# Moving eight small copies of v and halving one block transfer at the start of a fused attention and feed-forward kernel

## The chip, the cores and the metric

The kernel runs on one core of one Trainium2 chip. The metric is the device time of one execution in microseconds (us); the median of several executions is compared. TensorE (PE in the profile) multiplies matrices, VectorE is DVE, ScalarE is ACT, GpSimd is POOL, and SyncE (SP) issues nearly all DMA transfers. Each engine works through its own list of instructions in order and waits at an instruction until what it needs is there.

## The reference

Two blocks follow each other. The first is attention over 8 batches and 8 heads, with 576 positions of 64 numbers, in which every score that lies more than `tau` under the maximum of its row is dropped. The second is a feed-forward block on the 4608 resulting rows of 512 numbers.

```python
scores = scale * np.matmul(q, k.transpose(0, 1, 3, 2))
thresh = np.max(scores, axis=-1, keepdims=True) - tau
scores = np.where(scores >= thresh, scores, -1000000000.0)
attn = softmax(scores)                     # exp, divided by the sum of the row
attn_out = np.matmul(attn, v)              # (8, 8, 576, 64)
x = attn_out.transpose(0, 2, 1, 3).reshape(4608, 512)
h = x @ w_in                               # (4608, 1024), w_in arrives as 64-bit numbers
solu = h * softmax(h)
ln = (solu - mean) / sqrt(var + 1e-6) * g_ln
out = ln @ w_out                           # (4608, 512)
```

## The kernel before

**Rounds.** The attention is cut into 144 rounds (`slots`, 18 for each batch). A round handles 128 rows of scores for the two heads of a pair. Two rounds (r = 0 and r = 1) with the same batch, kind and pair `hp` make one unit; unit 0 is rounds 0 and 1, unit 1 is rounds 2 and 3, and unit 3, the fourth, is rounds 6 and 7. For one round the work passes over all engines:

- PE computes the scores of two heads into two banks of PSUM (`s_ps`, line 504), which are free only when the round before has been read.
- DVE finds the threshold of each row (line 526, result `nth`), once for each head.
- ACT turns the scores into differences from that threshold (line 541, called the ramp here) and takes the exponential with its row sum (line 550).
- One round later POOL normalises: two small operations on the sums (lines 557 and 558) and two multiplications of 128x576 (line 560). DVE then transposes the two results in blocks of 32x32 into `T` (line 571).
- When both rounds of a unit are transposed, SP sends `T` to `wT` in three transfers (`spread`, lines 592 and 594), which put the 32-row blocks on the partitions that the next product wants. `wT` has two buffers.
- Some rounds later PE multiplies `wT` with v (line 631, 72 matmuls), and ACT copies the result out of PSUM (line 664). These products fall due at fixed rounds: unit 0 in round 6, unit 1 in round 7, unit 2 in round 9, unit 3 in round 10.

**Weights.** Beside this, the first seventeen rounds convert the weights from 64-bit numbers piece by piece: a load on SP's queue (line 279), a scaled copy of the upper words (line 294 on ACT, or 298 on POOL or DVE), a mask on DVE (line 303), a conversion of the lower words on ACT (line 306), a merge on DVE (line 318) and an addition on POOL (line 328). Tables of numbers say in which round and at which of its places each of these is written.

**Order.** The program is written out by hand: `tc.manual_schedule()` keeps each engine's instructions in the order in which the code emits them. A round has places: its beginning (phase 0, ahead of its scores and thresholds), phase 1 (behind its exponentials), phase 2 (behind the normalisation of the round before) and its end (phase 3). `weigh(phase)` emits what the tables give for the number 4 * round + phase.

**Copies of v.** For batch 0 the product needs v twice: the upper half of the partitions also needs what the lower half holds, and the other way round. So 64 partitions times 2 heads times 256 numbers are copied across, in eight copies numbered 0 to 7: copies 0 and 1 serve unit 0, copies 2 and 3 unit 1, copies 4 and 5 unit 2, copies 6 and 7 unit 3. `VAT` gives the place of each copy and `VBY` its engine (0 is ACT, line 187; 1 is DVE, line 189; 2 is POOL, line 191).

```python
to = halves[b, hf]["v"][ROWS[r], 2 * pr : 2 * pr + 2, 4:8]
of = halves[b, hf]["v"][ROWS[1 - r], 2 * pr : 2 * pr + 2, 0:4]
if by == 0:
    nc.scalar.copy(out=to, in_=of)
elif by == 1:
    nc.vector.tensor_scalar(out=to, in0=of, scalar1=1.0, scalar2=None, op0=ALU.mult)
else:
    nc.gpsimd.tensor_scalar(out=to, in0=of, scalar1=1.0, scalar2=1.0, op0=ALU.mult, op1=ALU.mult)
```

**Halves of a unit.** From round 29 on (`START` is 30) `blocks` does not wait for the second round of a unit: it sends the half of r = 0 one place after the next round's exponentials, and the half of r = 1 when that is transposed. Before round 29 the whole unit is sent at once.

Of the kernel before, what the change touches and what calls it, by code (L numbers as in the profile page):

```python
# [20 lines left out]
def kernel(  # L21
# [161 lines left out]
    def copy_v(b, hf, pr, r, by):  # L183
# [7 lines that stand above are left out]
            nc.gpsimd.tensor_scalar(  # L191
                out=to, in0=of, scalar1=1.0, scalar2=1.0, op0=ALU.mult, op1=ALU.mult
            )
# [370 lines left out]
    def blocks(s):  # L564
        b, kind, hp, r = slots[s]
        key = (b, kind, hp)
        if r == 0:
            units[key] = dict(T=work.tile([P, 2, 2, NK, 2, 32], F32, tag="T", name="T"))
        T = units[key]["T"]
        for h, w in enumerate(live.pop(s)["w"]):  # L570
            nc.vector.transpose(  # L571
                out=T[:, :, r, :, h, :], in_=w.rearrange("p (c m x) -> p c m x", c=2, x=32)
            )
        if r == 1 or s >= START - 1:
            if r == 1:
                spread(key)
            else:
                jobs(MORE, s + 1, spread=lambda: spread(key, (0,)))

    def spread(key, rs=(0, 1)):  # L580

        kind = key[1]
        u = units[key]
        rs = [r for r in rs if r not in u.setdefault("spread", [])]
        if not u["spread"]:
            u["wT"] = work.tile([P, 2, 2, NK, 2, 32], F32, tag="wT", bufs=2, name="wT")
        u["spread"] += rs
        T = u["T"].rearrange("p c r m h x -> p c (r m h x)")
        to = u["wT"].rearrange("p g r m h x -> p g (r m h x)")
        rs = slice(64 * NK * rs[0], 64 * NK * (rs[-1] + 1))  # L590
        if kind < 2:
            nc.sync.dma_start(out=to[:, 1, rs], in_=T[32:96, :, rs])
            for half in range(2):
                nc.sync.dma_start(
                    out=to[ROWS[half], 0, rs], in_=T[96 * half : 96 * half + 32, :, rs]
                )
            return
        for g in range(2):
            for half in range(2):
                of = 64 * half + 32 * g  # L600
                nc.sync.dma_start(out=to[ROWS[half], g, rs], in_=T[of : of + 32, :, rs])
# [355 lines left out]
        "turn": (1, 0),  # L957
    }
    SPLIT = {30: 0, 32: 30, 34: 6, 36: 5, 38: 16, 40: 30, 42: 7, 44: 23, 46: 11}
    LATER, KEPT = 47, (3, 4)  # L960
    SEVEN = {0: 21, 1: 21, 2: 24, 3: 25, 5: 25, 4: 26, 7: 26, 6: 29}
    PIECE = {0: (-1, 1, 3, 6, 7, ), 1: (-1, 3, 5, 10, 11, ), 2: (-1, 8, 11, 14, 15, ), 3: (3, 12, 15, 18, 19, ), 4: (4, 15, 18, 21, 25, ), 5: (7, 20, 23, 26, 27, ), 6: (11, 23, 25, 30, 31, ), 7: (13, 27, 31, 34, 35, ), 8: (23, 31, 35, 38, 39, ), 9: (23, 35, 39, 42, 43, ), 10: (29, 39, 43, 46, 47, ), 11: (35, 43, 47, 50, 51, ), 12: (39, 49, 51, 54, 55, ), 13: (43, 52, 55, 58, 59, ), 14: (43, 55, 59, 62, 63, ), 15: (55, 59, 63, 66, 67, )}
    RAW = {0: 0, 1: 1, 2: 2, 3: 3, 4: 0, 5: 1, 6: 2, 7: 3, 8: 0, 9: 1, 10: 2, 11: 3, 12: 0, 13: 1, 14: 2, 15: 0}
    QUEUE = {0: 1, 1: 0, 2: 0, 3: 0, 4: 0, 5: 0, 6: 0, 7: 0, 8: 0, 9: 0, 10: 0, 11: 0, 12: 0, 13: 0, 14: 0, 15: 0}
    UNIT = {0: 0, 1: 2, 2: 2, 3: 2, 4: 1, 5: 2, 6: 1, 7: 1, 8: 1, 9: 0, 10: 1, 11: 1, 12: 1, 13: 1, 14: 0, 15: 0}
# [6 lines left out]
    LAG = {1: 2, 3: 1, 5: 1, 9: 1, 11: 1, 17: 0, 21: 0, 23: 1, 25: 1}  # L972
    FETCH = {0: 10, 1: 8, 2: 8, 3: 11, 4: 15, 5: 15, 6: 13, 7: 17, 8: 17, 9: 19, 10: 21, 11: 25, 12: 0, 13: 0, 14: 3, 15: 5}
    VHALF = (0, 1)
    VAT = {0: 15, 1: 15, 2: 19, 3: 19, 4: 31, 5: 31, 6: 34, 7: 34}
    VBY = {0: 2, 1: 2, 2: 2, 3: 2, 4: 0, 5: 0, 6: 0, 7: 0}
    LOAD2 = {0: 20, 1: 17, 2: 24, 3: 21, 4: 31, 5: 31, 6: 32, 7: 34}
    TURN2 = {0: 23, 1: 24, 2: 27, 3: 28, 4: 33, 5: 34, 6: 36, 7: 37}
    ENDS2 = {0: 30, 1: 28, 2: 42, 3: 44}
# [6 lines left out]
    def jobs(table, r, **do):  # L986
        for name, (phase, n) in table.items():
            if name in do:
                when = (begin, early, middle, late)[phase].setdefault(r + n, [])
                when.insert(0 if name in ("attended", "out") else len(when), do[name])  # L990
# [254 lines left out]
    START = 30  # L1245
# [70 lines left out]
    with tc.manual_schedule():  # L1316
# [40 lines left out]
        for x in range(NW):  # L1357
            def copies(x):
# [5 lines left out]
                (weight_load, weight_a, weight_b, weight_c, weight_gain, copies),  # L1364
                (*PIECE[x], MOVE.get(x, PIECE[x][4])),
            )
            for n, job, when in jobs_of:
                weights.setdefault(when, []).append((n, x, job))

        for x, when in VAT.items():  # L1370
            of = 0, VHALF[x // 4], x // 2 % 2, x % 2
            weights.setdefault(when, []).append(
                (6, x, lambda _, of=of, by=VBY[x]: copy_v(*of, by))
            )
# [85 lines left out]
        def attend_some(n):  # L1460
            key, steps = pv[0]
            if sum(1 for _ in zip(range(n), steps)) < n or n > 144:
                pv.clear()
                jobs(MORE, rnd, attended=lambda: done_with(key))

        def steady_round(due):
# [46 lines left out]
        while True:  # L1513
# [71 lines left out]
            if rnd - 1 in live:  # L1585
                blocks(rnd - 1)
# [47 lines left out]
```

## Time and profile before

| | |
|---|---|
| median of 3 runs | 846.54 us (844.78 to 851.36) |
| the profiled execution | 848.12 us, its span 846.3 us |
| PE busy | 799.6 us, 94% of the span |
| DVE, ACT, POOL busy | 674.5, 605.0, 574.2 us |
| HBM read, written | 45.09 MB, 9.44 MB |

The profile lists for each engine how long it was busy; its views show groups of instructions, windows of time, the instructions in order of time (the timeline) and the chain of work that ended last, followed back from the end. In the timeline a row starts with the start and the length in us, then come engine, line, operation, the tile that is written and the tile that is read, and a count; a bracket says how long the engine had been idle just before and whose result ended that. A row with a count merges several instructions of one kind. "issue" is idle time in which the engine waited for nothing that the profile shows. SPq rows are the times in which SP issues a transfer, not the transfer itself.

### The profile page before, as it was taken

How to read it: one execution, taken by the hardware profiler on the slowest of the kernel's cores; microseconds unless marked ns; L12 is line 12 of the kernel's file. 1: busy time of each engine (PE TensorE's matmuls, PEld its weight loads, DVE VectorE, ACT ScalarE, POOL GpSimd, SP SyncE). 2: the span in 40 equal slices, each digit the busy share in tenths (PEclk: the TensorE clock that was granted, in tenths of full speed). 3: DMA queues.
4: the chain of work that ended last, by engine and by line, in shares of the span. 5: the costliest groups of instructions: out<-in, count | busy, mean ns of one | idle time of the engine just before them, and what ended most of it. 6: DMA issues, size and time to landing. Idle time of an engine off the chain costs nothing.

```text
span 846.3 us, 36895 instructions
## 1 busy us (share of the span) xinstructions
PE 799.6 (94%) x15345; PEld 554.4 (66%) x15345; DVE 674.5 (80%) x1323; ACT 605.0 (71%) x1218; POOL 574.2 (68%) x1036
## 2 busy tenths in 40 slices
PE   5569889999999999999999999999999999999997
PEld 3346667766665666666777876666676876666556
DVE  5799869878789698979798698979688888787362
ACT  6799868767777686878686787778586687876231
POOL 4979767866867667677766768686666768574330
PEclk9789999999999999999999999999999999999999
DMA  8989788988787687968787677877687666555122
GB/s 252 256 219 253 189 204 212 236 222 211 220 244 216 174 224 211 242 190 218 205 230 208 195 207 220 231 206 199 192 218 222 180 183 201 150 138 139 42 52 52
DMA packets 99768, 166.40 MB, mean 197 GB/s; under 512 B 18504, under 2 KB 47184, under 8 KB 99600
## 3 DMA queue, kind: packets, MB, share of 16 engines
q1 hardware_dynamic: 98688, 162.95, 71.1%
q8 instruction: 121, 1.98, 1.0%
q10 hardware_dynamic: 912, 1.08, 0.5%
q14 instruction: 47, 0.39, 0.1%
HBM read 45.09 MB, written 9.44 MB: 64 GB/s over the span
## 4 chain that ended last, share of the span: by engine, by line
PE 82%; ACT 5%; POOL 3%; DMA 3%; issue 3%; DVE 2%; SPq 1%; DVEq 0%; POOLq 0%; ACTq 0%
PE ov L1195 22%; PE h L747 17%; PE s_ps L504 15%; PE ov L631 13%; PE o_ps L1195 6%; PE h L771 5%; ACT w L541 2%; PE h_ps L1061 2%; DMA wT<-T 2%; DMA v<-in_v_dram 1%; ACT w L550 1%; POOL w L560 1%; PE pv L631 1%; DVE w L526 1%; PE s_ps L372 1%
## 5 line engine op out<-in xcount | busy, mean ns | idle before, releaser
L541 ACT ACTIVATE w<-s_ps,nth 128x576 f32<-128x576 f32 x282 | 199.6, 741 | 141.4 <-DVE nth L526 136.2
L526 DVE CUSTOM_DVE_ANT_0 w<-s_ps,tau_t 128x576 f32<-128x576 f32 x282 | 201.4, 750 | 51.8 <-PE s_ps L504 40.7
L560 POOL TENSOR_SCALAR w<-w,sm 128x576 f32<-128x576 f32 x288 | 214.6, 757 | 14.3
L1195 PE MATMUL ov<-w,uT 64*64 64x256 f32 x3456 | 220.5, 379 | 2.8 <-issue 2.8
L571 DVE STREAM_TRANSPOSE T<-w 128x576 f32<-128x576 f32 x288 | 207.4, 755 | 19.2 <-POOL w L560 18.4
L550 ACT ACTIVATE w<-w,ntau 128x576 f32<-128x576 f32 x288 | 219.7, 768 | 0.0
L504 PE MATMUL s_ps<-kT,qT 64*64 64x512 f32 (+1 forms) x2048 | 174.8, 418 | 20.1 <-ACT w L541 17.9
L1195 PEld LDWEIGHTS ov<-w,uT 64*64 64x64 f32 x3456 | 158.3, 134 | 49.1 <-issue 13.6
L631 PEld LDWEIGHTS ov<-wT,v 64*64 64x64 f32 x4752 | 132.6, 133 | 33.5 <-issue 18.7
L631 PE MATMUL ov<-wT,v 64*64 64x128 f32 (+1 forms) x4752 | 137.6, 259 | 0.2
L557 POOL TENSOR_SCALAR sm<-sm 128x2 f32<-128x2 f32 x144 | 45.9, 319 | 134.9 <-ACT w L550 130.3
L558 POOL TENSOR_TENSOR sm<-sm,mone 128x2 f32<-128x2 f32 x144 | 103.5, 719 | 12.0
L504 PEld LDWEIGHTS s_ps<-kT,qT 64*64 64x64 f32 x2048 | 72.0, 137 | 51.0 <-ACT w L541 23.7
L747 PE MATMUL h<-w,xh 64*64 64x512 f32 x832 | 103.4, 593 | 0.5 <-POOL mark L110 0.4
L1150 DVE TENSOR_SCALAR u<-u,rs,nb 128x1024 f32<-128x1024 f32 x31 | 29.8, 961 | 49.6 <-ACT V L1144 49.6
L1195 PE MATMUL o_ps<-w,uT 64*64 64x256 f32 x1088 | 65.5, 377 | 0.8 <-ACT xh L664 0.5
L747 PEld LDWEIGHTS h<-w,xh 64*64 64x64 f32 x832 | 38.6, 133 | 40.5 <-issue 23.1
L1195 PEld LDWEIGHTS o_ps<-w,uT 64*64 64x64 f32 x1088 | 49.1, 133 | 19.1 <-issue 5.2
L550 ACT ACTIVATION_READ_ACCUMULATOR w<-w,ntau 128x1 f32 x288 | 55.7, 193 | 0.0
L1177 DVE STREAM_TRANSPOSE uT<-V 128x1024 f32<-128x1024 f32 x36 | 44.0, 1221 | 14.2 <-DMA V<-u 4.9
L747 PE MATMUL h<-k,sum 64*64 64x512 f32 x312 | 50.6, 589 | 0.0
L1144 ACT ACTIVATE V<-u,nb,rs 128x1024 f32<-128x1024 f32 x36 | 44.7, 1241 | 5.2 <-POOL nb L1122 5.2
(134 smaller groups left out, 1017.0 us busy)
## 6 DMA issues: line engine op xcount, KB each, us to landing
wT<-T SPq DMA_DIRECT2D x132, 288.0 KB, 4.8
wT<-T SPq DMA_DIRECT2D x256, 144.0 KB, 4.0
out_dram<-ob SPq DMA_DIRECT2D x71, 128.0 KB, 4.3
V<-u SPq DMA_DIRECT2D x136, 64.0 KB, 2.0
wT<-T SPq DMA_DIRECT2D x14, 576.0 KB, 5.5
q<-in_q_dram SPq DMA_DIRECT2D x24, 288.0 KB, 4.6
q<-in_k_dram SPq DMA_DIRECT2D x24, 288.0 KB, 4.5
v<-in_v_dram SPq DMA_DIRECT2D x12, 576.0 KB, 5.6
```

What stands on the lines that cost most here:

```text
L504: nc.tensor.matmul(out=ps[h][ROWS[y], ks], lhsT=lhsT, rhs=d["kT"][ROWS[h], ks], start=True, stop=True,)
L526: nc.vector.tensor_tensor_reduce(out=w, in0=ps[:, 0:S], in1=(zero if loose else tau_t).to_broadcast([P, S]), scale=1.0, scalar=BIG, op0=AL ...
L541: nc.scalar.activation(out=d["w"][x], in_=d["w"][x] if d["loose"] else d["ps"][x][:, 0:S], func=AF.Prelu, bias=d["nth"][x], scale=-1.0, al ...
L550: nc.scalar.activation(out=w, in_=w, func=AF.Exp, bias=ntau, scale=1.0, accum_out=sm[:, x : x + 1])
L557: nc.gpsimd.tensor_scalar(out=sm, in0=sm, scalar1=1e-9, scalar2=None, op0=ALU.add)
L558: nc.gpsimd.tensor_tensor(out=sm, in0=sm, in1=mone, op=ALU.pow)
L560: nc.gpsimd.tensor_scalar(out=w, in0=w, scalar1=sm[:, x : x + 1], scalar2=1.0, op0=ALU.mult, op1=ALU.mult)
L571: nc.vector.transpose(out=T[:, :, r, :, h, :], in_=w.rearrange("p (c m x) -> p c m x", c=2, x=32))
L631: nc.tensor.matmul(out=to, lhsT=d["v"][ROWS[u], (h0 + h - u) % 4 if b > 1 else h0 + h, m ^ 4 * u if m < 8 and b < 2 else m,], rhs=rhs, sta ...
L747: mm = nc.tensor.matmul(out=h[ROWS[y], 512 * bank : 512 * bank + 512], lhsT=x[ROWS[r], ROWS[y]], rhs=w[ROWS[r]], start=c == 0 and (n, r, k ...
L1144: nc.scalar.activation(out=V, in_=u, func=AF.Identity, bias=nb, scale=rs)
L1195: nc.tensor.matmul(out=to[ROWS[z], 0:256], lhsT=d["uT"][ROWS[r], m].rearrange("p y x -> p (y x)"), rhs=w2[ROWS[r], m ^ r, 256 * z : 256 * ...
```

## The change

Two things change. The eight copies get other places and partly other engines (`VAT`, `VBY`), and a unit whose first round is in `SOONER` (round 6, which is the fourth unit, unit 3) is sent in two halves, as the later units are. In `PIECE` only trailing commas go. Nothing else moves.

| copy | serves unit | before | now |
|---|---|---|---|
| 0 | 0 | POOL, end of round 3 | DVE, beginning of round 3 |
| 1 | 0 | POOL, end of round 3 | ACT, round 2, phase 1 |
| 2 | 1 | POOL, end of round 4 | DVE, beginning of round 4 |
| 3 | 1 | POOL, end of round 4 | POOL, end of round 3 |
| 4 | 2 | ACT, end of round 7 | POOL, end of round 8 |
| 5 | 2 | ACT, end of round 7 | ACT, beginning of round 8 |
| 6 | 3 | ACT, round 8, phase 2 | ACT, round 7, phase 1 |
| 7 | 3 | ACT, round 8, phase 2 | ACT, round 8, phase 2 |

```diff
@@ blocks
-        if r == 1 or s >= START - 1:
+        if r == 1 or s >= START - 1 or s in SOONER:
             if r == 1:
                 spread(key)
             else:
                 jobs(MORE, s + 1, spread=lambda: spread(key, (0,)))
@@ tables
+    SOONER = (6,)
...
-    VAT = {0: 15, 1: 15, 2: 19, 3: 19, 4: 31, 5: 31, 6: 34, 7: 34}
-    VBY = {0: 2, 1: 2, 2: 2, 3: 2, 4: 0, 5: 0, 6: 0, 7: 0}
+    VAT = {0: 12, 1: 9, 2: 16, 3: 15, 4: 35, 5: 32, 6: 29, 7: 34}
+    VBY = {0: 1, 1: 0, 2: 1, 3: 2, 4: 2, 5: 0, 6: 0, 7: 0}
```

What this does to POOL's list in rounds 3 and 4 (minus is before, plus is now):

```order
@@ -28,10 +28,9 @@
 L560 TENSOR_SCALAR w<-w,sm 128x576 x2
 L328 TENSOR_TENSOR w_74<-w_74,em 128x512
-L191 TENSOR_SCALAR v<-v 64x2x256 x2
+L191 TENSOR_SCALAR v<-v 64x2x256
 L557 TENSOR_SCALAR sm<-sm 128x2
 L558 TENSOR_TENSOR sm<-sm,mone 128x2
 L560 TENSOR_SCALAR w<-w,sm 128x576 x2
 L328 TENSOR_TENSOR w_74<-w_74,em 128x512
-L191 TENSOR_SCALAR v<-v 64x2x256 x2
 L298 TENSOR_SCALAR em<-raw 128x512
 L328 TENSOR_TENSOR w_74<-w_74,em 128x512
```

Of the four copies that stood between POOL's normalisations one is left, ahead of the normalisation of round 3.

ACT's list from the ramp of round 7 (line 541) to that of round 9, before:

```order
48 L541 ACTIVATE w<-s_ps,nth 128x576 x2
49 L550 ACTIVATE w,sm<-w,ntau 128x576 x2
50 L664 COPY xh<-pv 128x2x2x64
51 L294 ACTIVATE em<-raw 128x512
52 L306 ACTIVATE w_75<-raw 128x512
53 L187 COPY v<-v 64x2x256 x2
54 L541 ACTIVATE w<-s_ps,nth 128x576 x2
55 L550 ACTIVATE w,sm<-w,ntau 128x576 x2
56 L187 COPY v<-v 64x2x256 x2
57 L306 ACTIVATE w_75<-raw 128x512
58 L541 ACTIVATE w<-s_ps,nth 128x576 x2
```

and now:

```order
49 L541 ACTIVATE w<-s_ps,nth 128x576 x2
50 L550 ACTIVATE w,sm<-w,ntau 128x576 x2
51 L187 COPY v<-v 64x2x256
52 L664 COPY xh<-pv 128x2x2x64
53 L294 ACTIVATE em<-raw 128x512
54 L306 ACTIVATE w_75<-raw 128x512
55 L187 COPY v<-v 64x2x256
56 L541 ACTIVATE w<-s_ps,nth 128x576 x2
57 L550 ACTIVATE w,sm<-w,ntau 128x576 x2
58 L187 COPY v<-v 64x2x256
59 L306 ACTIVATE w_75<-raw 128x512
60 L541 ACTIVATE w<-s_ps,nth 128x576 x2
```

Two copies still lie between the ramps of rounds 7 and 8, no longer side by side, and one instead of two between those of rounds 8 and 9.

SP's list around the fourth unit:

```order
 L594 DMA wT<-T 64x1x1152 x2
 L279 DMA raw<-in_moe_w_out_dram 128x512
-L592 DMA wT<-T 128x1x1152
-L594 DMA wT<-T 64x1x1152 x2
+L592 DMA wT<-T 128x1x576
+L594 DMA wT<-T 64x1x576 x2
+L592 DMA wT<-T 128x1x576
+L594 DMA wT<-T 64x1x576 x2
 L279 DMA raw<-in_moe_w_out_dram 128x512
 L132 DMA k<-in_k_dram 128x2x256
```

Three transfers have become six of half the size, with nothing between the two halves. On DVE one copy stands ahead of the threshold step of round 3 and one ahead of that of round 4; on ACT one more stands in round 2, ahead of a conversion of weights (line 306).

More of the change, by code (lines that the diff above doesn't have):

```diff
@@ L959 @@
     SPLIT = {30: 0, 32: 30, 34: 6, 36: 5, 38: 16, 40: 30, 42: 7, 44: 23, 46: 11}
+    SOONER = (6,)
     LATER, KEPT = 47, (3, 4)
     SEVEN = {0: 21, 1: 21, 2: 24, 3: 25, 5: 25, 4: 26, 7: 26, 6: 29}
-    PIECE = {0: (-1, 1, 3, 6, 7, ), 1: (-1, 3, 5, 10, 11, ), 2: (-1, 8, 11, 14, 15, ), 3: (3, 12, 15, 18, 19, ), 4: (4, 15, 18, 21, 25, ), 5: (7, 20, 23, 26, 27, ), 6: (11, 23, 25, 30, 31, ), 7: (13, 27, 31, 34, 35, ), 8: (23, 31, 35, 38, 39, ), 9: (23, 35, 39, 42, 43, ), 10: (29, 39, 43, 46, 47, ), 11: (35, 43, 47, 50, 51, ), 12: (39, 49, 51, 54, 55, ), 13: (43, 52, 55, 58, 59, ), 14: (43, 55, 59, 62, 63, ), 15: (55, 59, 63, 66, 67, )}
+    PIECE = {0: (-1, 1, 3, 6, 7), 1: (-1, 3, 5, 10, 11), 2: (-1, 8, 11, 14, 15), 3: (3, 12, 15, 18, 19), 4: (4, 15, 18, 21, 25), 5: (7, 20, 23, 26, 27), 6: (11, 23, 25, 30, 31), 7: (13, 27, 31, 34, 35), 8: (23, 31, 35, 38, 39), 9: (23, 35, 39, 42, 43), 10: (29, 39, 43, 46, 47), 11: (35, 43, 47, 50, 51), 12: (39, 49, 51, 54, 55), 13: (43, 52, 55, 58, 59), 14: (43, 55, 59, 62, 63), 15: (55, 59, 63, 66, 67)}
     RAW = {0: 0, 1: 1, 2: 2, 3: 3, 4: 0, 5: 1, 6: 2, 7: 3, 8: 0, 9: 1, 10: 2, 11: 3, 12: 0, 13: 1, 14: 2, 15: 0}
```

## The prediction

> **What bounds the kernel now.** First the page's busy times and the windows, to see where time is still to be had. Columns of the windows: length, busy time (and count) of PE, its weight loads, DVE, ACT and POOL, granted clock of PE, busy share of the DMA engines, GB/s.
>
> ```profile
> PE 799.6 (94%) x15345; PEld 554.4 (66%) x15345; DVE 674.5 (80%) x1323; ACT 605.0 (71%) x1218; POOL 574.2 (68%) x1036
> ...
> 0.00:30.00 30.00, 17.15 (x369) 11.23 (x369) 19.69 (x42) 21.47 (x50) 17.14 (x34) 0.89 0.90 259
> 30.00:60.00 30.00, 19.32 (x314) 13.12 (x312) 24.28 (x47) 25.87 (x57) 23.97 (x32) 0.77 0.83 218
> 60.00:90.00 30.00, 25.71 (x468) 17.93 (x472) 27.05 (x55) 28.53 (x59) 26.96 (x40) 1.00 1.00 246
> 420.00:540.00 120.00, 119.79 (x2284) 89.44 (x2282) 102.18 (x205) 90.25 (x178) 83.25 (x154) 1.00 0.76 209
> ```
>
> Late in the kernel PE is busy for 119.79 of 120 us; nothing of the change lies there. In the first 60 us it is busy for 17.15 + 19.32 = 36.5 us, and all eight copies lie there. So the question is how much earlier the rounds after the tenth start, and whether that lead survives until PE alone sets the pace.
>
> Next the chain of waits through 27 to 39 us (start, length, what):
>
> ```profile
> 27.68 0.94 POOL v L191
> 28.69 0.69 POOL v L191
> 29.45 0.24 POOL sm L557
> 33.52 0.67 POOL v L191
> 34.26 0.61 POOL v L191
> ```
>
> Four copies of v stand on the path itself, and POOL's work behind them. The timeline shows what they hold up, the step from round 5 to round 6:
>
> ```profile
> 31.68 0.76 ACT L550 ACTIVATE w<-w,ntau 128x576 f32<-128x576 f32 x1
> 34.95 0.65 POOL L298 TENSOR_SCALAR em<-raw 128x512 f32<-128x512 f32 x1
> 36.91 0.23 POOL L557 TENSOR_SCALAR sm<-sm 128x2 f32<-128x2 f32 x1
> 38.82 1.50 DVE L571 STREAM_TRANSPOSE T<-w 128x576 f32<-128x576 f32 x2 [3.75 <-POOL w L560]
> 41.71 0.74 DVE L526 CUSTOM_DVE_ANT_0 w<-s_ps,tau_t 128x576 f32<-128x576 f32 x1
> 42.55 1.42 ACT L541 ACTIVATE w<-s_ps,nth 128x576 f32<-128x576 f32 x2 [4.01 <-DVE nth L526]
> ```
>
> The exponentials of round 4 end at 32.44 (31.68 + 0.76), but POOL takes their sums only at 36.91. So DVE idles 3.75 us before it can transpose round 4, the threshold of round 6 stands behind that in DVE's list, and ACT idles 4.01 us for it. That is the largest hole here, and POOL makes it.
>
> **The change part by part, round 2 to round 6.** These rows price the copies that move to ACT and DVE:
>
> ```profile
> 24.68 1.42 ACT L541 ACTIVATE w<-s_ps,nth 128x576 f32<-128x576 f32 x2
> 28.18 0.73 DVE L303 TENSOR_SCALAR em<-raw 128x512 int32<-128x512 int32 x1
> 45.45 0.38 DVE L303 TENSOR_SCALAR em<-raw 128x512 int32<-128x512 int32 x1
> 25.66 1.50 DVE L571 STREAM_TRANSPOSE T<-w 128x576 f32<-128x576 f32 x2 [0.40 <-POOL w L560]
> 29.61 1.42 ACT L541 ACTIVATE w<-s_ps,nth 128x576 f32<-128x576 f32 x2 [0.72 <-DVE nth L526]
> 34.53 1.41 ACT L541 ACTIVATE w<-s_ps,nth 128x576 f32<-128x576 f32 x2
> 51.19 1.25 ACT L187 COPY v<-v 64x512 f32<-64x512 f32 x2
> ```
>
> *On ACT*, copy 1 costs 1.25 / 2 = 0.62 us, ahead of the ramp of round 3 (24.68), which follows without a gap. *On DVE* the trace has no copy of v. Nearest is line 303, one input and one output with 512 numbers in a partition as the copy has: 0.38 us at 45.45, where POOL is idle, 0.73 us at 28.18, where POOL works. POOL works in rounds 3 and 4, so I take 0.73 for each and 0.38 as the lower end. DVE has 0.40 us of idle time between the two (at 25.66), so the threshold of round 4 comes 2 x 0.73 - 0.40 = 1.06 later, about 1.0, and with it the ramp of round 4, which waits for exactly that (0.72 us at 29.61). ACT's own 0.62 runs beside this and does not add. From 29.61 to 34.53 ACT has no gap, so the ramp of round 5 is 1.0 later too. This is the price of the change.
>
> [...]
>
> *On POOL* three copies go. With the gaps behind them they take 29.45 - 28.69 = 0.76 us in round 3 and 34.95 - 33.52 = 1.43 us in round 4, together 2.19. Is POOL still late without them? It would reach the sums of round 4 at 36.91 - 2.19 = 34.72; the exponentials end at 32.44 + 1.0 = 33.4. So POOL stays the later one by 1.3 us, the delay on ACT is covered, and the whole 2.19 counts: transposes of round 4 at 36.63, ramp of round 6 at 42.55 - 2.19 = 40.36. ACT was free 4.01 us before 42.55, at 38.54, now at 39.5: in time.
>
> **Round 7.** Between the rounds PE has its own list: scores of round 6, product of unit 0, scores of round 7.
>
> ```profile
> 37.76 3.35 PE L631 MATMUL pv<-wT,v 64*64 64x128 f32 x72
> 43.35 0.41 PE L504 MATMUL s_ps<-kT,qT 64*64 64x64 f32 x4 [2.23 <-ACT w L541]
> 46.06 0.76 DVE L526 CUSTOM_DVE_ANT_0 w<-s_ps,tau_t 128x576 f32<-128x576 f32 x1 [0.23 <-PE s_ps L504]
> 46.86 1.42 ACT L541 ACTIVATE w<-s_ps,nth 128x576 f32<-128x576 f32 x2
> ```
>
> The product follows the scores of round 6, which follow the ramp of round 5: 1.0 later, from 38.8 to 42.1. The scores of round 7 therefore start at 42.1 instead of 43.35, 1.25 us earlier and not 2.19. DVE already waits for them (0.23 at 46.06). So I take a lead of 1.3 us at the ramp of round 7; with DVE copies of 0.38 it is 1.3 + 2 x (0.73 - 0.38) = 2.0.
>
> **Rounds 8 and 9.**
>
> ```profile
> 52.47 1.37 ACT L541 ACTIVATE w<-s_ps,nth 128x576 f32<-128x576 f32 x2
> 55.37 1.24 ACT L187 COPY v<-v 64x512 f32<-64x512 f32 x2
> 55.44 0.22 POOL L557 TENSOR_SCALAR sm<-sm 128x2 f32<-128x2 f32 x1 [1.55 <-ACT w L550]
> 57.23 1.36 ACT L541 ACTIVATE w<-s_ps,nth 128x576 f32<-128x576 f32 x2
> ```
>
> Ahead of the ramp at 52.47 ACT has two copies before and two now: no change. Ahead of the ramp of round 9 at 57.23 it has one less: 1.24 / 2 = 0.62, so the lead grows to 1.9 us. Copy 4, now on POOL at the end of round 8, fits into the 1.55 us in which POOL idles before 55.44 (a copy took 0.61 to 0.94 there); without that cover it would cost at most its 0.94 at the product of unit 2.
>
> **The halves.** SP's issues, the landing, and who waits:
>
> ```profile
> 54.16 2.90 SPq L594 DMA_DIRECT2D wT<-T  x2
> 62.26 2.07 PE L631 MATMUL pv<-wT,v 64*64 64x128 f32 x66 [0.87 <-DMA wT<-T]
> 64.49 0.37 ACT L664 COPY xh<-pv 128x256 f32<-128x256 f32 x1 [0.18 <-PE pv L631]
> ```
>
> The last whole transfer is issued by 57.06 (54.16 + 2.90), and the product of unit 3 waits for its blocks until 62.26. But ACT, which needs the result at 64.49, waits only 0.18 us for it, and in the window from 60 to 90 ACT is busy for 28.53 of 30 us: the wait of PE hides behind ACT. So the halves bring 0 to 0.2 us by themselves. What they do is keep the lead: unsplit, the blocks would not come 1.9 earlier with certainty, as the DMA engines are full from 60 on (share 1.00). The first half now leaves a round earlier. Behind it in SP's list stand only the second half and later loads, and SP was idle there, so nothing is held up. I count 0.
>
> **The sum.** -2.19 on POOL becomes -1.3 at round 7 through PE, and -0.62 on ACT in round 8: 1.9 us. The profiled execution would go from 848.12 to 846.2, and the median from 846.54 to 844.6 us. (The profiled execution lies 1.6 us over the median, within the 844.78 to 851.36 of the runs.) Nothing later gives it back if loads and products shift along with the rounds.
>
> **The rivals.**
>
> *The lead is lost to the DMA.* The engines are full from 60 to 90, and a load gates ACT there:
>
> ```profile
> 87.68 0.67 ACT L306 ACTIVATE w<-raw 128x512 int32<-128x512 uint32 x1 [1.17 <-DMA raw<-in_moe_w_out_dram]
> ```
>
> If bytes and not issues set when that load lands, the rounds come earlier and then wait for it: at most 0.2 us remain, 846.3. Against it: from 30 to 60 the share is 0.83, so 30 x 0.17 = 5 us of room take an earlier issue.
>
> *More than summed.* The half that leaves a round early takes load off the full stretch, the 1.17 us at 87.68 go as well and the 0.18 of ACT: 1.9 + 1.35 = 3.25, 843.3.
>
> *Slower: the copies on DVE wait out POOL's steps.* Round 4's threshold is the place. If each of the two copies waits for a whole addition (1.27 us, the first row below) before its own 0.38, each costs 1.65.
>
> ```profile
> 35.56 1.27 POOL L328 TENSOR_TENSOR w<-w,em 128x512 int32<-128x512 int32 x1
> 40.93 0.86 DVE L303 TENSOR_SCALAR em<-raw 128x512 int32<-128x512 int32 x1
> ```
>
> Then PE's product of unit 0 is 2 x 1.65 - 0.40 = 2.9 later and ends at 44.0, after 43.35: round 7 is 0.65 late instead of early. It decides from a copy of 1.32 us on (2 x 1.32 - 0.40 = 2.24, the room of PE). If the 0.62 of round 8 is then lost behind the scores of round 9, the time is 846.54 + 0.65 = 847.2. For it speaks that line 303 doubles when POOL works; against it that line 303 took no more than 0.86 beside POOL's multiplications (second row).
>
> **How the numbers follow.** Forecast 0.58; lost to the DMA 0.18; more than summed 0.13; slower 0.11. The forecast's own range is 1.3 to 2.6 us (no saving in round 8; copies of 0.38), 843.9 to 845.2. The range of 842.6 to 847.3 takes in all four cases with 0.7 below the fastest for what the rows do not show. One per cent, about what a measurement of this kernel can tell from no change, is 8.5 us; no case comes near. I leave 0.03 for faster and 0.03 for slower, as another phase of the rounds can change PE's granted clock (0.77 from 30 to 60 against 1.00 later), and 0.94 for the same.
>
> **What would show it.** In the profile of the changed kernel: the idle time of DVE before the transposes of round 4 falls from 3.75 to between 0.6 and 1.2 us, and that of ACT before the ramp of round 6 from 4.01 to about 1; the ramp of round 6 is near 40.4, that of round 7 near 45.6, that of round 9 near 55.3. The two DVE copies last 0.4 to 0.75 us. The product of unit 3 waits for no transfer. After 100 us the instructions stand 1.9 us earlier. It is wrong if round 6 is early and round 11 is not (a transfer or PE took the lead back), if the DVE copies last over 1.3 us, or if POOL waits for exponentials at round 4.

## The result, and the profile after

The changed kernel takes 843.12 us (median of 22 runs, 841.5 to 849.89), the kernel before 846.66 us (22 runs, 843.56 to 851.36). The ratio is 0.9968, with a 95% interval of 0.9953 to 0.9983: 0.32% or 2.7 us less, and by the interval 1.4 to 4.0 us less. (The two medians lie 3.5 us apart; the ratio compares the whole groups.) The forecast was 844.6 within 842.6 to 847.3, a gain of 1.9 us and a time within 1% of before. The interval holds the forecast's 1.9 and also the 3.25 of the rival "more than summed"; the time alone doesn't decide between them. The profiled execution took 841.82 us.

**Which executions to compare.** The windows of the changed kernel have the columns of those shown for before:

```profile
0.00:30.00 30.00, 18.63 (x367) 12.55 (x369) 19.74 (x44) 21.82 (x51) 17.86 (x34) 0.85 0.91 261
30.00:60.00 30.00, 22.04 (x380) 15.04 (x376) 26.68 (x51) 27.55 (x59) 25.22 (x34) 0.69 0.92 252
...
420.00:540.00 120.00, 119.76 (x2310) 88.75 (x2306) 103.39 (x207) 90.87 (x181) 82.89 (x152) 1.00 0.76 212
```

More work of every engine lies in the first 60 us (PE 40.7 us instead of 36.5), and the late stretch is PE's as before, 119.76 of 120 us. But a part of this is no effect of the change. The timeline of before, then that of the changed kernel, with POOL's normalisation of rounds 2, 10 and 18:

```profile
24.07 0.71 POOL L558 TENSOR_TENSOR sm<-sm,mone 128x2 f32<-128x2 f32 x1
65.03 0.87 POOL L558 TENSOR_TENSOR sm<-sm,mone 128x2 f32<-128x2 f32 x1
111.40 0.71 POOL L558 TENSOR_TENSOR sm<-sm,mone 128x2 f32<-128x2 f32 x1
```

```profile
23.59 0.87 POOL L558 TENSOR_TENSOR sm<-sm,mone 128x2 f32<-128x2 f32 x1
63.05 0.71 POOL L558 TENSOR_TENSOR sm<-sm,mone 128x2 f32<-128x2 f32 x1
106.76 0.71 POOL L558 TENSOR_TENSOR sm<-sm,mone 128x2 f32<-128x2 f32 x1
```

At round 2 the two are 0.48 us apart already. A second execution of the kernel before (label e0_before_again, below) has its round 2 at 23.58, so the first profile of before simply began half a microsecond late. From here on "lead" is the difference of these rows less the difference at round 2: 65.03 - 63.05 - 0.48 = 1.50 us at round 10, and 111.40 - 106.76 - 0.48 = 4.16 at round 18.

**The hole at round 6.** The second execution of before, and then the changed kernel, in their timelines:

```profile
29.27 0.71 POOL L558 TENSOR_TENSOR sm<-sm,mone 128x2 f32<-128x2 f32 x1
30.09 1.62 POOL L560 TENSOR_SCALAR w<-w,sm 128x576 f32<-128x576 f32 x2
36.43 0.23 POOL L557 TENSOR_SCALAR sm<-sm 128x2 f32<-128x2 f32 x1
38.33 1.50 DVE L571 STREAM_TRANSPOSE T<-w 128x576 f32<-128x576 f32 x2 [3.76 <-POOL w L560]
42.07 1.42 ACT L541 ACTIVATE w<-s_ps,nth 128x576 f32<-128x576 f32 x2 [4.02 <-DVE nth L526]
```

```profile
23.32 0.62 ACT L187 COPY v<-v 64x512 f32<-64x512 f32 x1
23.46 0.42 DVE L189 TENSOR_SCALAR v<-v 64x512 f32<-64x512 f32 x1
28.60 0.42 DVE L189 TENSOR_SCALAR v<-v 64x512 f32<-64x512 f32 x1
28.73 0.87 POOL L558 TENSOR_TENSOR sm<-sm,mone 128x2 f32<-128x2 f32 x1
29.70 1.98 POOL L560 TENSOR_SCALAR w<-w,sm 128x576 f32<-128x576 f32 x2
30.42 0.72 DVE L318 SCALAR_TENSOR_TENSOR em<-em 128x512 int32<-128x512 int32 x1
35.03 0.22 POOL L557 TENSOR_SCALAR sm<-sm 128x2 f32<-128x2 f32 x1
36.92 1.50 DVE L571 STREAM_TRANSPOSE T<-w 128x576 f32<-128x576 f32 x2 [2.12 <-POOL w L560]
38.02 4.00 PE L631 MATMUL pv<-wT,v 64*64 64x128 f32 x72
40.68 1.42 ACT L541 ACTIVATE w<-s_ps,nth 128x576 f32<-128x576 f32 x2 [1.86 <-DVE nth L526]
41.75 1.60 PE L504 MATMUL s_ps<-kT,qT 64*64 64x64 f32 x16
44.93 1.35 ACT L541 ACTIVATE w<-s_ps,nth 128x576 f32<-128x576 f32 x2
```

POOL reaches the sums of round 4 at 35.03 instead of 36.43, 1.40 us sooner, and the transposes and the ramp of round 6 follow it. DVE still waits 2.12 us for POOL there, ACT 1.86 for DVE (the prediction expected 0.6 to 1.2, and about 1): the hole is smaller, not gone. The scores of round 7 start (41.75) as the product of unit 0 ends (38.02 + 4.00), so PE has no room left there. But ACT does not wait for them: its ramp of round 7 (44.93) has no idle time ahead of it. That ramp stood at 46.86 before, so its lead is 46.86 - 44.93 - 0.48 = 1.45 us.

The chain of waits of the changed kernel through the same stretch as before:

```profile
27.36 0.94 POOL v L191
...
35.03 0.23 POOL sm L557
```

One copy of v is left on the path where there were four.

**Round 9 on.** The timeline of the changed kernel from there (issues of SP, then who uses what they bring):

```profile
48.53 0.73 SPq L592 DMA_DIRECT2D wT<-T  x1
52.25 1.25 SPq L594 DMA_DIRECT2D wT<-T  x2
54.94 1.42 ACT L541 ACTIVATE w<-s_ps,nth 128x576 f32<-128x576 f32 x2
58.53 2.07 PE L631 MATMUL pv<-wT,v 64*64 64x128 f32 x66 [0.24 <-DMA wT<-T]
59.62 1.42 ACT L541 ACTIVATE w<-s_ps,nth 128x576 f32<-128x576 f32 x2 [0.34 <-DVE nth L526]
62.45 0.36 ACT L664 COPY xh<-pv 128x256 f32<-128x256 f32 x1
84.28 0.74 ACT L306 ACTIVATE w<-raw 128x512 int32<-128x512 uint32 x1
```

The first half of unit 3 leaves at 48.53, the second is issued by 53.50 (52.25 + 1.25), and the long run of the product starts at 58.53 instead of 62.26. ACT takes the result without a wait, and the 1.17 us that ACT waited at 87.68 before don't appear at 84.28.

### The profile page after: what moved, and what is told of

It is laid out like the page before. It is cut to its first block, busy times and chain, and to the rows that moved or that the text cites. A ratio compares the mean times of both kernels' runs of the same rounds, so it can differ in the third digit from the quotient of the medians.

```text
span 840.0 us, 36900 instructions
## 1 busy us (share of the span) xinstructions
PE 798.8 (95%) x15345; PEld 551.3 (66%) x15345; DVE 674.5 (80%) x1325; ACT 605.0 (72%) x1218; POOL 573.7 (68%) x1034
## 3 DMA queue, kind: packets, MB, share of 16 engines
q8 instruction: 121, 1.98, 1.0%
## 4 chain that ended last, share of the span: by engine, by line
PE 81%; ACT 6%; POOL 4%; issue 2%; DMA 2%; DVE 2%; SPq 1%; DVEq 0%; POOLq 0%; ACTq 0%
PE ov L1196 22%; PE h L747 18%; PE s_ps L504 15%; PE ov L631 14%; PE o_ps L1196 7%; PE h L771 4%; ACT w L541 2%; ACT w L550 2%; DMA wT<-T 2%; POOL w L560 1%; PE h_ps L1062 1%; POOL sm L558 1%; POOL w L328 1%; PE pv L631 1%; DVE T L571 1%
```

## The experiments

Each run compares its kernel with the kernel before on the same chip; such ratios are of groups of 10 to 12 runs against 29 to 35 (the change itself, 22 against 22). The table puts together what all executions showed. Leads are worked out as above, in us, against the first profile of before, at the normalisation of the round named; "ACT waits" is the wait of line 664 for the product of unit 3; "half clock" says whether PE was granted less than 0.8 in a window of 2 us between 63 and 67 us.

| run | round 8 | 10 | 12 | 18 | 30 | ACT waits | half clock | ratio (95%) |
|---|---|---|---|---|---|---|---|---|
| first profile of before | 0 | 0 | 0 | 0 | 0 | 0.18 | no | |
| e0_before_again | -0.01 | -0.01 | -2.05 | -0.93 | -1.68 | 1.59 | yes | |
| e4_load15_earlier | 0.01 | 0.03 | -2.03 | -0.97 | -1.70 | 1.62 | yes | 1.0013 (0.9999 to 1.0028) |
| e7_filler_round10 | 0.00 | 0.00 | -3.98 | -1.58 | -1.61 | 3.83 | yes | 1.0007 (0.9995 to 1.0019) |
| e12_filler_free_bank | 0.02 | 0.03 | -2.36 | -1.26 | -0.84 | 0.61 | no | 1.0001 (0.9984 to 1.0018) |
| e11_extra_copy_pool | -0.71 | -0.70 | -2.61 | -1.39 | -1.60 | 1.31 | yes | 1.0010 (0.9995 to 1.0026) |
| e6_last_four | -0.07 | 0.13 | -0.18 | 0.45 | 0.68 | 0.29 | no | 0.9987 (0.9966 to 1.0008) |
| e2_halves_only | 0.15 | 0.16 | 0.26 | 1.24 | -0.01 | none | no | 1.0002 (0.9986 to 1.0018) |
| e5_first_four | 1.50 | 1.50 | 0.95 | 1.77 | 1.71 | 0.74 | no | 0.9963 (0.9942 to 0.9983) |
| e10_first_four_again | 1.48 | 1.49 | 1.07 | 1.68 | -0.07 | 0.37 | no | 0.9994 (0.9975 to 1.0013) |
| e1_copies_only | 1.30 | 1.51 | 1.27 | 1.89 | 1.27 | 0.21 | no | 0.9983 (0.9966 to 1.0000) |
| e9_four_halves | 1.50 | 1.75 | 1.78 | 2.80 | 3.17 | none | no | 0.9963 (0.9943 to 0.9982) |
| the change | 1.30 | 1.50 | 1.58 | 4.16 | 3.42 | none | no | 0.9968 (0.9953 to 0.9983) |
| e8_after_again | 1.30 | 1.50 | 1.59 | 3.61 | 2.42 | none | no | 0.9971 (0.9950 to 0.9992) |

The history up to round 10 repeats to 0.03 us in the kernels that share it. Beyond it two executions of one program differ: the two of before by 2.05 us at round 12, the changed kernel's two by 0.55 at round 18 and 1.00 at round 30. So reasons are read from the traces up to round 12, with care up to 18, and the worth of a part over the whole kernel from the times.

### The same kernels a second time

Nothing is edited in e0_before_again (one run, 848.13 us) and e8_after_again (843.42 us, median of 12).

> The kernel before, profiled a second time, to see which differences between two traces come from the change. 'Lead' is how much earlier than in the first profile of before POOL starts its second operation on the sums (line 558) of a given round. If the stalls seen after round 75 and the 1.60 us of PE near 87 us belong to the kernel, the lead is within 0.3 us at rounds 8, 14, 20 and 40. If they belong to the single execution, it jumps there by 1 to 3 us. The 1.17 us that ACT waits for a load of weights near 87 us should be there again (0.8 to 1.6) if the DMA backlog makes it.

> The changed kernel, profiled again and timed beside the others. If its gain beyond the 1.4 us of the copies belongs to the kernel, the lead counted from round 2 is again over 3 us at round 20, there is no stretch of half clock between 60 and 100 us, and the product of unit 3 waits under 1 us for its blocks. If it is a matter of the single execution, the lead at round 20 is between 1.3 and 2.5. The median is 2 to 4 us under before.

The changed kernel's history repeats (its lead at round 20 is 3.61, over 3 as expected, though its product waits 1.35 us for blocks and not under 1). The kernel before's doesn't, and the wait for the load near 87 us is not there again. The product of unit 3 in the timeline of the first execution of before:

```profile
60.95 0.44 PE L631 MATMUL pv<-wT,v 64*64 64x128 f32 x4 [1.12 <-DMA wT<-T]
```

and, of the second, the product and the copy behind it:

```profile
61.28 0.43 PE L631 MATMUL pv<-wT,v 64*64 64x128 f32 x4 [1.91 <-DMA wT<-T]
62.25 2.91 PE L631 MATMUL pv<-wT,v 64*64 64x128 f32 x66 [0.54 <-DMA wT<-T]
65.42 0.37 ACT L664 COPY xh<-pv 128x256 f32<-128x256 f32 x1 [1.59 <-PE pv L631]
```

The second execution is 0.49 us ahead up to there, but the long run of the product starts at the same time (62.25 and 62.26). So PE waits longer for the blocks, 1.91 + 0.54 = 2.45 us against 1.12 + 0.87 = 1.99. The product then takes 2.91 us instead of 2.07, and ACT waits 1.59 us for it where the first profile had 0.18. The windows of this execution say why the product is slower (columns as above):

```profile
61.00:63.00 2.00, 1.18 (x32) 0.97 (x36) 1.64 (x4) 2.00 (x6) 1.90 (x4) 1.00 1.01 319
63.00:65.00 2.00, 2.00 (x58) 2.00 (x51) 1.82 (x3) 0.83 (x3) 1.83 (x3) 0.58 1.12 249
65.00:67.00 2.00, 2.00 (x24) 1.35 (x21) 0.07 (x1) 1.58 (x4) 1.90 (x4) 0.57 0.99 299
```

The granted clock falls to a half for about 3.4 us right behind PE's idle time (the shares of 0.58 and 0.57 are 0.84 + 0.86 us lost, at a half clock 3.4 us). The product behind it runs slower; with the longer wait the lead at round 12 is -2.05. In the table this half clock stands in four of the seven executions that have whole blocks and not the first four copies (in one of the other three, e12, PE's idle time was filled). The first profile of before is one without it.

### The copies without the halves, and the halves without the copies

e1_copies_only has the change's `VAT` and `VBY` and no halves; e2_halves_only the reverse.

```diff
 e1_copies_only, against the changed kernel
-    SOONER = (6,)
+    SOONER = ()
 e2_halves_only, against the kernel before
-        if r == 1 or s >= START - 1:
+        if r == 1 or s >= START - 1 or s in SOONER:
+    SOONER = (6,)
```

> The eight copies as in the changed kernel, the fourth unit sent whole. Theory (two parts: the copies give about 1.9 us by round 8, the halves relieve the DMA engines and take away the wait for weights near 87 us): lead 1.8 to 2.3 at round 8, the product of unit 3 waits for its blocks, ACT still waits about 1 us for the weights of round 14, lead 1.5 to 2.3 at round 40, time about 2 us under before. Rival (the earlier rounds alone relieve the DMA engines): no wait in round 14, lead 3.3 to 4 at round 40, as in the changed kernel.

> Only the fourth unit in halves, the copies as before. Theory: lead 0 to 0.2 at round 10, as ACT sets the pace there; the product of unit 3 no longer waits; the wait for weights in round 14 shrinks and the lead at round 40 is 1 to 1.7 us. Rival (halves alone do nothing, as the prediction counted them): lead 0 to 0.2 at round 40 as well, time as before.

The copies alone have the whole lead of the change up to round 10 (1.51) and lose 0.24 of it by round 12; the changed kernel loses none. Neither expectation held as it stood: the lead at round 8 was 1.30 and not 1.8 to 2.3, and ACT waited 0.63 us for the load. The halves alone bring 0.16 us by round 10, and ACT doesn't wait for the product. In the timeline of the kernel with halves only:

```profile
60.07 2.54 PE L631 MATMUL pv<-wT,v 64*64 64x128 f32 x70
64.07 0.36 ACT L664 COPY xh<-pv 128x256 f32<-128x256 f32 x1
88.22 0.69 ACT L306 ACTIVATE w<-raw 128x512 int32<-128x512 uint32 x1 [2.12 <-DMA raw<-in_moe_w_out_dram]
```

The long run of the product starts 2.2 us earlier than the 62.26 of the first profile. But ACT's wait for the load near 88 us is 2.12 us, longer than the 1.17 of before. So the theory that the halves shrink that wait fails, and it isn't they that took it away in the changed kernel. Over the whole time the halves alone give 1.0002 (0.9986 to 1.0018): at most 1.2 us of 846, and zero fits.

### The load ahead of ACT's wait, one round earlier

The load of the last piece of weights moves from the end of round 13 to the end of round 12.

```diff
-    PIECE = {..., 15: (55, 59, 63, 66, 67)}
+    PIECE = {..., 15: (51, 59, 63, 66, 67)}
```

> The kernel before with one number changed: the last piece of the weights is loaded one round earlier, at the end of round 12. It tests by itself what the wait of ACT and DVE for that load in round 14 costs. If that wait is what the changed kernel gained beyond 1.9 us: no wait there, lead 0 up to round 13, then 1.2 to 1.7 us at round 40. Rival (PE's stall of 1.60 us in front of the scores of round 15 is what counts, and it is no matter of this load): the wait goes, the lead at round 40 stays under 0.5 us.

This missed its aim. Its execution had the half clock, as that of e0_before_again, and then no wait for the load; but e0_before_again, with the load where it was, had no such wait either. Both were 2 us late by then. The ratio, 1.0013 (0.9999 to 1.0028), shows no gain from an earlier load.

### Which copies count

e5_first_four moves copies 0 to 3 and leaves 4 to 7; e6_last_four the reverse. e10_first_four_again is e5_first_four once more.

```diff
 e5_first_four and e10_first_four_again
+    VAT = {0: 12, 1: 9, 2: 16, 3: 15, 4: 31, 5: 31, 6: 34, 7: 34}
+    VBY = {0: 1, 1: 0, 2: 1, 3: 2, 4: 0, 5: 0, 6: 0, 7: 0}
 e6_last_four
+    VAT = {0: 15, 1: 15, 2: 19, 3: 19, 4: 35, 5: 32, 6: 29, 7: 34}
+    VBY = {0: 2, 1: 2, 2: 2, 3: 2, 4: 2, 5: 0, 6: 0, 7: 0}
```

> Only copies 0 to 3 in their new places; copies 4 to 7 and the fourth unit as before. Leads are against the first profile of before and counted from the lead at round 2, since the start of single executions differs by 0.5 us. Theory (POOL's hole between rounds 5 and 6 is all that these four are worth): 1.3 to 1.6 us from round 4 to round 8, with no further growth at round 9; 0.9 to 1.6 at round 14. Rival (the four are worth nothing beyond round 10, as DVE or ACT is the slowest there anyway): under 0.5 at round 10.

> Only copies 4 to 7 in their new places; copies 0 to 3 and the fourth unit as before. Theory as predicted (one copy less on ACT ahead of the ramp of round 9): lead 0 up to round 8, 0.6 at round 9, and it stays. Rival, seen in the changed kernel's trace, where the lead went from 1.78 to 2.52 at round 9 and back to 1.98 at round 10: DVE takes it back at once, lead 0 to 0.3 from round 10 on, and the time is that of before.

> The first four copies alone, a second time, beside the kernel with the halves on the same chip. If the halves add a gain of their own on top of the copies: 0.5 to 2 us slower than with them (844 to 846 us), a lead of 1.3 to 1.5 us at the eighth to tenth round, under 2.2 at the eighteenth. If the halves count nothing: the same time within 0.3 us and the same lead at the eighteenth round.

The first four have the whole 1.50 us of round 10. The last four have a lead of 0.68 at round 9 and 0.13 at round 10. Their timeline, the ramps of rounds 9 and 10:

```profile
56.28 1.42 ACT L541 ACTIVATE w<-s_ps,nth 128x576 f32<-128x576 f32 x2
60.96 1.42 ACT L541 ACTIVATE w<-s_ps,nth 128x576 f32<-128x576 f32 x2 [0.34 <-DVE nth L526]
```

In e0_before_again these two stand at 56.74 and 60.90. ACT gains 0.46 at round 9 by the copy that is gone, and then waits for DVE, which didn't get faster. Over the whole time e6_last_four gives 0.9987 (0.9966 to 1.0008), not told from 1. The first four gave 0.9963 once and 0.9994 the second time; the two intervals only just overlap. That is how far two such groups of ten runs can lie apart.

### One copy more on POOL

e11_extra_copy_pool is the kernel before with copy 3 made twice, both times on POOL at the end of round 4.

```diff
+        weights.setdefault(19, []).append((6, 3.5, lambda _: copy_v(0, 0, 1, 1, 2)))
```

> The kernel before with one more copy on GpSimd, a repeat of copy 3 in the fifth round, so the suspected cost is larger by one. If GpSimd's own time sets the stretch up to the ramp of round 6: VectorE and ScalarE stand idle 0.6 to 0.95 us longer ahead of it, and the lead from the seventh round on is -0.6 to -0.95 us; the whole time is longer by the same (ratio about 1.001). If another engine sets it, lead 0 +-0.1 and no change of the time.

The timeline of this kernel at the hole:

```profile
32.97 2.05 POOL L191 TENSOR_SCALAR v<-v 64x512 f32<-64x512 f32 x3
37.07 0.23 POOL L557 TENSOR_SCALAR sm<-sm 128x2 f32<-128x2 f32 x1
38.97 1.50 DVE L571 STREAM_TRANSPOSE T<-w 128x576 f32<-128x576 f32 x2 [4.45 <-POOL w L560]
42.70 1.42 ACT L541 ACTIVATE w<-s_ps,nth 128x576 f32<-128x576 f32 x2 [4.46 <-DVE nth L526]
```

POOL's three copies there take 2.05 us where its two took 1.35 in e0_before_again, 0.70 more. The sums come 0.64 later than in e0_before_again (36.43), the ramp 0.63 later (42.07), in an execution that began 0.07 us earlier, so the lead is -0.70 to -0.71 from round 4 to round 10. DVE idles 0.69 us longer (4.45 against 3.76), ACT 0.44 (4.46 against 4.02), the latter a little under what was expected. The copy more on POOL cost what it lasted there, 0.70 us: this settles that POOL makes the hole. The time, 1.0010 (0.9995 to 1.0026), agrees with 0.7 us and doesn't prove it.

### Filling PE's idle time

Both kernels are the kernel before with matmuls that nothing reads, ahead of the product of unit 3, where PE waits for blocks. The first wrote them to the banks of the scores, the second to a free pair.

```diff
+                    if rnd == 10:
+                        for x in range(12):
+                            turn(live[rnd]["spare"], x % 7, lambda r, y: ident[ROWS[r], ROWS[r]])
...
+                    if rnd == 10:
+                        tag, tile_f = take("fill")
+                        fill = {0: tile_f[:, 0:512], 1: tile_f[:, 512:1024], "base": 0}
+                        for x in range(12):
+                            turn(fill, x % 8, lambda r, y: ident[ROWS[r], ROWS[r]])
+                        pairs_free.insert(0, tag)
```

> The kernel before, with 48 small matmuls that nobody reads (64x64, about 1.5 us) ahead of the product of unit 3 in round 10, where PE idles for its blocks. It leaves the wait for the blocks alone and takes away only PE's idleness. Theory (what the halves and the earlier rounds bring beyond the copies is that PE is not idle so long that its clock is halved afterwards): granted clock 1.00 from 61 to 68 us, where the second profile of before had 0.50 for 3 us; ACT waits under 0.5 us for the product of unit 3 (1.59 there); the median 0 to 1.5 us under before. Rival (the late landing costs by itself): ACT waits 1 us or more at a clock of 1.00.

> The kernel before with 48 matmuls of 64x64 that nothing reads, into a free pair of PSUM banks, ahead of the product of unit 3, in the time that TensorE stands waiting for its blocks. If the idle time ahead of that product is what brings the half clock at 63 to 67 us: granted clock 1.00 through 61 to 68 us, ScalarE's wait for the product under 0.5 us, and a lead at the fourteenth round that is not below -0.5 (the two runs of before with the half clock had -2.1). If the half clock has nothing to do with that idle time: 0.50 for 3 to 4 us there again in about every second execution. If the filler only delays the product: a wait longer by up to 2.4 us at full clock. One profile speaks for one execution only.

The first was badly built. Its timeline:

```profile
61.79 0.33 PE L372 MATMUL s_ps<-ident 64*64 64x64 f32 x4 [2.34 <-ACT w L541]
64.01 3.70 PE L631 MATMUL pv<-wT,v 64*64 64x128 f32 x70
```

The filler itself waited 2.34 us for ACT to free the banks of the scores, so it filled nothing, pushed the product back by some 1.7 us, and the half clock came all the same. It says only that a later product there is paid in full (ACT waits 3.83 us, the lead falls to -3.98). The timeline of the second:

```profile
62.16 2.07 PE L631 MATMUL pv<-wT,v 64*64 64x128 f32 x66 [0.57 <-DMA wT<-T]
64.39 0.37 ACT L664 COPY xh<-pv 128x256 f32<-128x256 f32 x1 [0.61 <-PE pv L631]
66.10 0.66 PE L504 MATMUL s_ps<-kT,qT 64*64 64x512 f32 x4 [1.42 <-issue]
```

Here the idle time was filled, PE kept its full clock (1.00 in each window of 2 us from 61 to 69 us), and the product took 2.07 us. The clock is what the theory of the half clock expected, in one execution; ACT's wait, 0.61, is a little over the expected 0.5. But the lead at round 12 was -2.36 all the same: PE stood 1.42 us in the middle of the scores behind it and waited for nothing that the profile shows. So the filler removed one loss and another was there, and the time (1.0001) didn't move.

What came ahead of the half clock can be counted in all traces together. In the first profile of before all changes of the granted clock lie whole steps of 3.41 us apart (among them 43.46, 46.87, 53.70, 57.11 and 94.66 us), and in the changed kernel too, at other places (41.63, 48.45, 55.28 us). The other twelve traces have such steps as well, each at its own places. In the last stretch of 3.41 us between two steps ahead of the half clock at 63 to 67 us, PE had worked for 1.48 to 1.66 of the 3.41 us (e4, e0, e11, e7). Where the clock stayed at 1.00, the least that PE had worked in a stretch there is 1.92 (e10); it is 2.12 in the first profile of before (from 60.52 to 63.94 us), 2.61 with the filler (e12, from 59.85 to 63.27) and 2.1 or more with halves. So in these executions the half clock stands behind a stretch in which PE was busy for less than half. That the wait for the blocks made such a stretch in some of them and not in others because of where the steps lay is an estimate from these sums. The filler is the one test by an edit, in one execution.

### First four copies and the halves

e9_four_halves leaves copies 4 to 7 where they were before, and has the rest of the change.

> Copies 0 to 3 in their new places and the halves of the fourth unit; copies 4 to 7 stay on ScalarE in the old rounds 31 and 34. If the gain is that of the first four copies plus the vanished wait of unit 3's product, and the last four are worth nothing over the whole: lead over the first profile of before 1.3 to 1.5 at the eighth to tenth round and 3 or more at the eighteenth, no wait of ScalarE for unit 3's product, and a time equal to the changed kernel's within 0.2% (842 to 844 us), ratio 0.996 to 0.997. If the last four carry a part (0.62 us), 0.6 us more than the changed kernel. If the halves are worth nothing, the time of the first four copies alone, which was 844.39 us.

Its ratio, 0.9963 (0.9943 to 0.9982), is the changed kernel's; its median, 844.45, is 1.2 us under that of e10_first_four_again on the same chip. ACT has no wait for unit 3's product, and at round 18 the lead is 2.80, a little under the expected 3. The last four copies are not needed for the gain. It is no faster than the changed kernel as far as these runs can tell.

## Why the prediction was right, and where its steps were off

**The copies leave POOL: right place, size too large.** The step was 2.19 us; the sums of round 4 came 1.40 sooner. The rows above have the rest. Three of POOL's steps last longer in the changed kernel: line 558 in rounds 2 and 3, 0.87 us instead of 0.71, and line 560 in round 3, 1.98 instead of 1.62. That is 0.16 + 0.16 + 0.36 = 0.68, and 2.19 - 0.68 = 1.51; the other 0.11 lies in steps that grow by 0.05 us or less. All six executions with copies 0 and 2 on DVE show these longer steps (0.81 to 0.87 and 1.98); the eight with them on POOL have 0.71 and 1.62. Only line 558 has a copy beside it. Of line 560 it is the second multiplication that is slow, 1.25 us instead of 0.74. It starts at 30.43 together with DVE's merge (line 318, at 30.42), which the copy has pushed there: in the first profile of before the merge started at 30.17, beside the first multiplication. So POOL got back less than the copies had lasted there, because its steps beside the copies and the merge lasted 0.68 us longer. The prediction counted only the slot of the copy. This is read from the timelines; no run moves one DVE instruction alone.

**The price on DVE: too large, and no harm.** A copy took 0.42 us and not 0.73, though POOL was working, so the lower end of 0.38 was the better one. The third rival (each copy waits out a step of POOL, 1.32 us or more) did not come about: each copy started at the end of a short step (line 557, 0.27 us), and it was POOL's step that grew. No copy met one of POOL's long steps, so what one costs there is not shown. In all six executions, in both rounds, line 558 ends 0.57 us behind the end of DVE's copy, and the slow multiplication of line 560 ends 0.53 us behind the merge. In the changed kernel's timeline above DVE's copy ran from 28.60 to 29.02, and POOL's step of line 558, begun at 28.73, ended at 29.60. It grew by 0.16 us, less than the 0.42 of the copy; by what means the one holds up the other the timelines do not show.

**Round 7: the number near, the limit another.** Forecast 1.3 us at the ramp of round 7, set by PE. It was 1.45, no less than the 1.39 at the ramp of round 6, and ACT worked through from 40.68 to 44.93 without waiting for PE. So PE took nothing from the lead. POOL had given only 1.40, and that this lies near 1.3 is luck. (The same ramp had no wait at 46.86 before either, as the prediction's own row shows.) The product of unit 0 started 0.74 us later, where 1.0 was forecast, but took 4.00 us instead of 3.35, with the granted clock at 0.50 up to 41.63 us (up to 40.05 before). With copies of 0.38 the prediction had allowed 2.0; that wasn't there, since POOL gave only 1.40.

**Round 9: right at its place, then lost.** The lead grew to 2.04 at round 9 (forecast 1.9) and fell to 1.50 at round 10. The term of 0.62 is the one most mis-sized: it is 0.0 to 0.1 (e1 against e5, and e6), and with the halves e9, which lacks it, is even 0.25 ahead of the change at round 10. In the changed kernel's timeline DVE has no idle time from the start of the thresholds of round 9 (54.08) to the end of those of round 10 (60.25), and the ramp of round 10 waits 0.34 us for it. A saving on ACT there had DVE behind it, and the prediction had not looked one round further.

**The halves count 0: the step that was wrong.** That the blocks would not come 1.9 us earlier unsplit was right: with whole blocks 0.24 to 0.55 us of the lead are lost between rounds 10 and 12 (e1, e5, e10), and none with halves (the change, e8, e9). But the prediction took ACT's wait of 0.18 us for the whole of what there was to gain. The six other executions with whole blocks and without the first four copies wait 0.29 to 3.83 us there, 1.59 in the one that differs in nothing. One profile had shown the case without the half clock. By the table the halves are worth 0.3 to 2.3 us at round 12 (0.26 in e2_halves_only, against 0 and -2.05 in the two executions of before), according to which case an execution falls into; by the times, anything from nothing to 1.2 us alone. Nor did the product quite wait for no transfer: 0.11 and 0.24 us here and 1.35 in e8_after_again, all hidden from ACT.

**More than 1.5 us by round 18.** From round 12 to round 18 the changed kernel gains another 2.58 us on the first profile of before. Some of it is gained with no change at all (1.12 in e0_before_again), since that profile lost time there, with ACT's 1.17 us for the load: from round 14 to 15 the changed kernel gains 1.16, and the six other executions without the first four copies and without the halves gain 1.11 to 1.16. From round 15 to 18 it gains another 1.16. There the windows of before show a half clock:

```profile
94.00:96.00 2.00, 1.78 (x22) 1.04 (x25) 0.68 (x2) 1.53 (x4) 1.07 (x3) 0.67 0.47 113
96.00:98.00 2.00, 2.00 (x47) 2.00 (x43) 1.92 (x5) 1.12 (x3) 2.00 (x3) 0.50 0.29 70
```

and of the changed kernel at the same work:

```profile
90.00:92.00 2.00, 1.94 (x55) 0.84 (x44) 1.41 (x2) 2.00 (x6) 0.95 (x3) 1.00 0.72 184
```

The changed kernel keeps its full clock there. But e1, e5 and e10 keep it too and gain only 0.61 to 0.82 from round 12 to 18. PE stood 1.1 to 1.4 us near 86 us there for no cause that the profile shows, which it did not in the changed kernel. How these parts add up stays open. The rival "more than summed" said that the halves relieve the full stretch of the DMA and the wait for the load goes. The wait did go, but not by the halves (e2_halves_only kept 2.12 us of it) and it is gone in executions of before that run late, too. So that mechanism is not shown, though the size came near.

**What stays.** Over the whole kernel the two runs of the change give 0.9968 and 0.9971. The copies are the part that the traces show without exception, 1.5 us by round 10; what the halves add, and why the kernel keeps more than 1.5 us in the end, is only bounded. So that the forecast of 1.9 lies in the interval is in part luck: it was 1.3 from PE's limit at round 7 and 0.62 from ACT at round 8, and neither set the time. The traces have 1.40 from POOL, nearly nothing from ACT, and something from the halves that the forecast put at nothing. The rival in which the lead is lost to the DMA falls: between rounds 10 and 12 the changed kernel loses nothing.

## What to carry to other kernels

Take a small step off the engine that makes the others wait, and count what its neighbours on that engine lose beside it: here three copies of 2.19 us in all gave back 1.40. Before an engine is named as the next limit, see whether anyone waits for it there. Follow a saving one round past the place where it appears, to the engine that is busy without a gap there. Before a wait is called hidden, look at more than one execution of the same kernel: 0.18 us in one was 1.6 in the next.

## What the runs showed of the hardware

- Two executions of one program differ by the granted clock of PE: from 65 to 67 us it was 1.00 in the first profile of before and 0.57 in e0_before_again. In the traces it is 1.00 or 0.50. In the first profile of before its 15 changes lie whole steps of 3.41 us apart, in the changed kernel its 7 do, with the steps at other places. Counted over the 14 traces by stretches of 3.41 us between the steps, it went from 1.00 to 0.50 behind 63 of the 66 stretches in which PE was busy for less than half, behind 6 of 38 with a share of 0.5 to 0.6, and behind none of 3167 with more; in the first profile of before alone these are 5 of 5, 2 of 5 and none of 226, in the changed kernel 2 of 3, 1 of 3 and none of 226. It came back only behind a stretch with a share over 0.8 (0.91 or more in these two). (The other three of the 66 each hold an unexplained gap of PE, of the kind below, of 1.7 to 2.1 us.) In e0_before_again PE worked for 1.50 of the 3.41 us ahead of the half clock, and its longest single wait was 1.91 us.
- Steps of POOL grew beside instructions of DVE. In the six executions with copies 0 and 2 on DVE, line 558 beside a copy takes 0.81 to 0.87 us instead of 0.71 and ends 0.57 us behind the copy, and line 560, whose second multiplication starts beside the merge, takes 1.98 instead of 1.62 and ends 0.53 behind the merge. No run moves one of these instructions alone.
- PE stood 1.1 to 1.6 us with nothing that the profile shows among the matmuls ahead of and of the scores (lines 372 and 504) near 86 to 88 us in before and in e1, e2, e5 and e10, and 0.5 us in e6, which stands 1.3 us more at 93.9; 1.4 us at 66 us in e12. The other executions lack it there. Near 120 to 125 us most executions have such a gap (1.83 us ahead of 123.50 in the first profile of before, 1.79 ahead of 119.84 in the changed kernel). No run tells its cause.
- A copy of 64x512 numbers took 0.42 us on DVE and 0.62 on ACT in the changed kernel, and 0.61 to 0.94 on POOL in the first profile of before.
